# A new hand-laid order for the first half of an S4 convolution and gated feed-forward kernel

## The chip, the cores and the metric

The kernel runs on one core of a Trainium2 chip. The metric is device time in microseconds (us), from the start of the execution to its end. A core has five engines that matter here: PE (TensorE, matrix products), DVE (VectorE), ACT (ScalarE), POOL (GpSimd) and SP (SyncE, which here only starts transfers). Each engine works through its own list of instructions in a fixed order and waits on semaphores for the others. Transfers between HBM and the on-chip memory are started by SP, ACT or POOL and carried out by 16 DMA engines.

## The reference

One block of a network: a layer norm with a modulation, a long convolution whose kernel comes from a diagonal state-space model, and a gated feed-forward part. Sizes are L = 2048 positions, D = 448 channels, N = 256 complex states for each channel, Df = 1792.

```python
mod = silu(c) @ w_mod                      # six rows: sa ca ga sb cb gb
h = layernorm(x) * (1 + ca) + sa
# the convolution's kernel, 448 x 2048, from 256 complex exponentials each:
P = exp((dt * A)[:, :, None] * l)          # D x N x L
K = einsum("dn,dnl,dn->dl", Cc, P, dB).real
y = irfft(rfft(h, 2L) * rfft(K, 2L))[:L] + h * Dskip
x = x + ga * y
h = layernorm(x) * (1 + cb) + sb
x = x + gb * ((gelu(h @ w_gate) * (h @ w_up)) @ w_down)
```

## The kernel before

The work falls into two halves.

The first half, up to about 387 us, makes the convolution. The exponentials are never formed in full: a position is split into two factors (32 by 64), so that K is a product of two small tables for each channel. The channels go in 56 steps of eight. For a step, PE forms the arguments (`x.mm` L638, `y.mm` L657, `ang` L675) from rows `lt` that SP loads (`lt0`, `lt1`, L620; eight of each, seven steps use one), ACT takes the exponential (L644, L662) and sine and cosine (L688, L692, after an absolute value `mag` at L680 on ACT or L683 on DVE), DVE multiplies magnitudes with phases (`tx` L721, `ty` L725), and PE sums over the states (`kgen` L748). Every second step is drained (`kev`, L480 on ACT or L482 on DVE) and given the first pass of its Fourier transform (`ka`, L771). Beside this the input's transform runs (`ua`, `ub` L984, with stores `ub.st` of `us` at L1001). For the first two groups of channels, 160 each, the spectra are then multiplied and transformed back (`k_fft`: load of constants `f.fc` L1081, load of the input's spectrum `f.ut` L1087 and L1089, `f.fwd` L1094, `f.pr` L1098, `f.inv` L1105, drain `f.z`, store `f.st` L1113).

The last 128 channels follow at about 350 us in `t_fft` (products at L1197 and L1200, PE at L1189, L1207 and L1216). Its results go to memory twice: as `y` (L1231), and, for the first block of positions, as `yb_d` (drain `t.s0` by L480, store `t.st` L1224) so that the reload `yi.l` (L1297) of that block can begin early, batch by batch, nine batches of two transfers. The last stage of the convolution for the first block (L1409 and after) needs all of them.

The second half is the feed-forward part in four blocks of positions: gate and up products on PE (`gate_up`, L1524 and L1530), GELU on ACT, the product on DVE, and the down projection (L1599, L1630). `w.ld` (L1332) loads its weights, `yi.ld` (L1278) the later blocks of `y`.

What sets the order: every operation is registered as a task with `add(name, ...)`; `Task.__init__` (L275) takes its place from the table `PLACE` (L40 to L262), by name and running count. `Plan.order` sorts all 2006 tasks by place, and `Plan.run` emits them one by one. A letter behind a number names the engine where a task may go to more than one: a for ACT, d for DVE, p for POOL, s for SP. Each engine runs its instructions in the order in which they are emitted, and a transfer is an instruction of the engine that starts it. Nothing in the table is a wait: waits come from the data and from buffers that are used in turn. Places below 1480 are those ahead of the gate tiles of the second block of positions; the text calls the n-th task of a name (from zero) `name#n`.

```python
at = PLACE[n][i]
self.at, e = int(at.rstrip("adps")), at[-1]
...
out = sorted(self.tasks, key=lambda t: t.at)
```

Of the kernel before, what the change touches and what calls it, by code (L numbers as in the profile page):

```python
# [40 lines left out]
    "anc": "119 123 138 176 166 197 210 239 264 304 319 337 348 357 435 461 483 471 498 486",  # L41
    "ang": "113 108 132 150 164 172 203 208 233 303 318 332 345 355 426 460 478 441 497 473 510 582 605 595 665 679 657 694 "
        "743 751 766 787 783 801 773 876 878 916 894 903 938 934 1004 1023 1012 1033 1041 1047 1112 1126 1140 1145 1169 "
        "1176 1196 1201",
    "as": "69a 58a 101d 98d 121d 126d 174a 167d 251d 255a 280d 289a 311d 324d 334d 353a",
    "bn": "45 50 46 47 10 14 11 12 230 231 235 232 161 163 189 219",
    "c.ai": "1250",
    "c.ak": "201",
    "c.au": "57",
    "c.c": "16",  # L50
    "c.ea": "59",
    "c.ih": "1254",
    "c.ld": "21",
    "c.rd": "78",
    "c.t1": "236",
    "co.adde": "1338 1339 1355 1364",
    "co.addl": "1383 1391 1419 1416",
    "co.addx": "1495 1510 1499 1522 1672 1712 1735 1684 1791 1803 1809 1801",
    "co.ca": "1405a 1415a 1444a 1438a",
    "co.cb": "1413d 1418a 1454a 1447a",  # L60
    "co.h0": "1397a 1401a 1431a 1433a",
    "co.h2": "1534a 1580a 1571a 1562a 1748a 1744d 1755a 1760d 1848d 1882a 1833a 1866a",
    "co.l0": "1402 1411 1437 1445",
    "co.l2": "1541 1585 1573 1577 1749 1751 1757 1761 1849 1885 1843 1876",
    "co.mme": "1321 1317 1346 1347",
    "co.mml": "1374 1380 1417 1378",
    "co.mmx": "1492 1506 1494 1509 1636 1699 1731 1645 1784 1797 1804 1788",
    "co.n": "1396 1400 1429 1426",
    "co.nx": "1527 1575 1549 1532 1745 1742 1747 1759 1821 1868 1829 1863",
    "co.rc": "1393 1399 1428 1425",  # L70
    "co.rcx": "1525 1739 1820",
    "co.rt": "1384 1394 1427 1420",
    "co.rtx": "1524 1737 1810",
    "co.xt": "1542 1586 1574 1578 1750 1752 1758 1762 1850 1886 1851 1877",
    "co.ta": "1404 1410 1432 1434",
    "co.tb": "1407 1414 1443 1446",
    "cos": "521 588 634 616 689 704 686 708 754 760 769 792 791 819 813 886 899 932 909 923 953 954 1014 1034 1030 1054 1046 "
        "1052 1117 1139 1144 1153 1173 1190 1199 1222",
    "cos2": "122 124 145 179 169 200 212 245 269 313 326 338 349 359 439 463 484 472 505 488",
# [3 lines left out]
    "d0": "175",  # L83
# [21 lines left out]
    "dsk": "193",  # L105
    "dt": "24",
# [4 lines left out]
    "ev.end": "1247",  # L111
    "ev.fp": "697",
    "ev.geg": "1462",
    "ev.pq": "1334",
    "ev.ps": "1451",
    "ev.ub": "385",
    "ev.w0": "1333",
    "f.fc": "726 746 779 808 818 833 881 888 926 944 962 1020 1049 1074 1089 1119 1134 1152 1164 1191",
    "f.fwd": "727 759 786 809 821 850 884 892 930 950 966 998 1015 1028 1056 1075 1095 1120 1136 1160 1206 1218",
    "f.inv": "750 771 794 817 844 864 897 924 948 961 984 1008 1025 1053 1068 1086 1110 1131 1150 1182 1214 1230",  # L120
    "f.pr": "749 765 788 816 838 851 895 904 931 952 983 999 1016 1029 1067 1083 1096 1121 1149 1178 1213 1221",
    "f.st": "831 780 857 866 907 893 941 946 979 1007 1003 1044 1061 1077 1109 1124 1135 1170 1198 1205 1241 1281",
    "f.ut": "698 758 774 805 820 841 883 891 929 920 964 980 1006 1026 1055 1048 1080 1103 1122 1147 1185 1157",
    "f.z": "755a 772d 812d 832a 865a 887d 908d 928a 949a 986d 993d 1009d 1027d 1066d 1085a 1098d 1111a 1132a 1155a 1183a "
        "1219a 1233d",
    "gs": "64 77",
    "gu": "1479 1497 1511 1519 1528 1539 1550 1561 1570 1579 1592 1612 1618 1628 1640 1647 1656 1665 1674 1682 1690 1702 "
        "1708 1717 1769 1773 1776 1790 1792 1800 1808 1814 1822 1830 1835 1844 1853 1862 1895 1898 1901 1907 1912 1919 "
        "1923 1929 1933 1946 1952 1958 1962 1969",
    "gu.g": "1430 1440 1448 1458 1467 1465 1473 1481 1502 1508 1521 1529 1540 1551 1563 1572 1582 1591 1600 1619 1629 1637 "  # L130
        "1650 1657 1666 1675 1683 1691 1705 1709 1718 1723 1774 1777 1785 1793 1798 1805 1816 1823 1831 1836 1845 1854 "
        "1867 1870 1899 1902 1908 1913 1920 1924 1930 1934 1947 1953 1960 1963 1970 1975",
    "gu.h0": "1478 1485 1515 1536 1558 1581 1595",
# [5 lines left out]
    "gu.m": "1439 1441 1456 1461 1469 1470 1476 1483 1505 1513 1526 1531 1546 1555 1565 1576 1590 1593 1605 1621 1633 1639 "  # L139
# [3 lines left out]
    "gu2": "1422 1423 1442 1457 1459 1464 1471 1472",  # L143
    "ka": "228 261 292 341 382 405 506 527 656 585 703 712 737 828 800 871 914 943 970 989 1057 1076 1125 1165 1187 1210 "
        "1237 1245",
    "kd": "227 250 291 340 374 404 450 504 590 577 700 711 736 827 798 863 902 927 968 988 1040 1072 1102 1148 1186 1209 "
        "1236 1239",
    "kev": "218d 224a 290d 317a 373d 394d 448a 490a 548d 569d 699d 707d 735d 806d 797d 858a 900a 918a 960d 975a 1037a 1071d "
        "1101a 1138a 1166a 1195a 1235a 1238d",
    "kgen": "141 177 191 216 253 277 271 316 300 360 375 393 414 419 476 485 520 535 552 563 626 643 669 690 715 718 748 763 "  # L150
        "777 790 815 830 855 885 910 911 933 959 955 974 1018 1019 1045 1065 1081 1099 1129 1133 1156 1163 1175 1193 1204 "
        "1220 1224 1232",
    "kout": "229a 266a 299d 342a 442d 407a 507a 544a 658a 598a 710a 738d 739a 843a 804a 877d 917a 945d 976a 994a 1070d 1094a "
        "1130a 1167a 1188a 1211a 1244d 1246a",
    "lt0": "61 112 302 369 561 744 852 1017",
    "lt1": "95 162 384 432 742 745 965 1060",
    "m.cp": "553a 604a 793d",
    "m.cp0": "41d",
    "m.ev": "42 63 68 568 614 799",
    "m.ld": "27 36 17 433 558 761",  # L160
    "m.mm": "34 52",
    "m.mq": "549 603 776",
    "m.mq0": "20",
    "m.sm": "554 613 795",
    "m.sm0": "55",
    "mag": "518a 587a 610a 597d 670a 680d 664a 705a 752d 756a 767a 789a 784a 810a 775a 879a 889d 921a 905a 913a 939a 935a "
        "1010a 1031a 1013d 1038a 1042a 1050a 1116d 1127a 1142a 1146a 1171a 1177a 1197a 1202a",
    "norm": "66 70 93 67 118 65 89 110 234 252 273 243 320 307 308 350",
    "p.A1": "2 90 314 502",
    "p.A2": "3 91 330 508",  # L170
    "p.A3": "25 154 346 487",
    "p.B1": "6 107 354 543",
    "p.B2": "22 149 391 580",
    "p.B3": "23 151 427 629",
    "p.C1": "28 102 420 500",
    "p.C2": "32 103 421 607",
    "p.D1": "29 142 418 581",
    "p.E1": "38 171 446 639",
    "p.E2": "39 199 491 684",
    "p.E3": "43 205 492 685",  # L180
    "p.G1": "35 128 436 615",
    "p.S1": "5 104 331 542",
    "p.S2": "8 114 366 565",
    "p.S3": "9 125 390 579",
    "p.S4": "37 168 444 638",
    "p.al": "1 15 259 451",
    "p.c0": "26a 159d 428d 632d",
    "p.c1": "44a 241d 511a 729d",
    "p.d0": "30 183 429 660",
    "p.d1": "53 309 539 807",  # L190
    "p.e0": "31d 240d 458a 678d",
    "p.e1": "56d 321a 584d 845d",
    "p.f0": "40 244 459 730",
    "p.f1": "60 322 611 875",
    "p.ld": "0 7 86 87 170 265 368 452",
    "p.put0": "49 301 475 814",
    "p.put1": "85 323 674 901",
    "pad": "48 247 181 695",
    "rcp": "54 248",
    "rstd": "51 242",  # L200
# [1633 lines left out]
```

## Time and profile before

| what | us |
|---|---|
| median of 3 runs | 783.3 |
| lowest and highest of them | 781.65, 783.98 |
| the profiled execution's own time | 783.97 |
| its span in the profile | 782.0 |
| PE, DVE, ACT busy in the span | 728.2, 590.7, 459.6 |

The profiled execution's own time lies 0.67 us above the median of the runs. Its span runs from the first to the last recorded instruction; 2 us lie around it. The share of an engine that is busy is an average over stages that differ much: in the first half three engines are near full at once, in the second PE alone. So the readings below go by stretch of the span. Rows of a timeline hold the start in us, the duration, the engine, the line and operation, and in brackets the idle time ahead of it with what ended it; an engine's name with a q (SPq, ACTq) is the issue of a transfer by it. Rows of the stretches hold, for each engine, the busy time and the number of instructions, then the clock that PE was granted (1 is full) and the load on the DMA engines. Rows of the chain of waits hold start, duration and what ran.

### The profile page before, as it was taken

Reading aid. Unit: us, or ns where it says so; the run is one execution under the profiler, and the core shown is the slowest. Engines: PE = TensorE matmul, PEld = TensorE weight load, DVE = VectorE, ACT = ScalarE, POOL = GpSimd, SP = SyncE. Lnnn points to the kernel's source line nnn. Section 1 sums busy time; section 2 is a strip of 40 time slices with the busy share of each in tenths; the row PEclk is TensorE's granted clock in tenths of the full one; section 3 lists DMA queues with packets and bytes.
Section 4 is the critical chain, followed back from the end, with each engine's and each line's share of the span. In section 5 each row is a group of like instructions: output and inputs, shape, how many; then the busy total and the mean of one; then the engine's idle time right before and its main releaser. Section 6 shows DMA issues by size and latency. Waiting matters only on the chain.

```text
span 782.0 us, 19039 instructions
## 1 busy us (share of the span) xinstructions
PE 728.2 (93%) x8166; PEld 443.6 (57%) x8166; DVE 590.7 (76%) x889; ACT 459.6 (59%) x615; POOL 8.4 (1%) x23
## 2 busy tenths in 40 slices
PE   3677889998899999989999999999999999999998
PEld 1234444444577777677774445444694446944477
DVE  6999999999899999979767952569774587034743
ACT  5899998999899999862554730233411334022330
POOL 0000000000000000001200000000000000000000
PEclk9999999999999999999999999999999999999999
DMA  8645569998887598888876884355337224013201
GB/s 264 190 140 177 143 159 273 254 300 248 210 237 243 161 258 244 238 303 238 253 234 227 281 217 132 130 177 168 140 66 224 95 95 135 14 48 98 79 2 60
DMA packets 103950, 139.87 MB, mean 179 GB/s; under 512 B 34388, under 2 KB 85492, under 8 KB 103866
## 3 DMA queue, kind: packets, MB, share of 16 engines
q1 hardware_dynamic: 100436, 132.53, 57.8%
q10 hardware_dynamic: 2950, 5.38, 2.1%
q8 instruction: 64, 1.05, 0.6%
q0 software_dynamic: 480, 0.75, 0.3%
q14 instruction: 20, 0.16, 0.1%
HBM read 100.39 MB, written 36.01 MB: 174 GB/s over the span
## 4 chain that ended last, share of the span: by engine, by line
PE 66%; ACT 9%; DMA 8%; DVE 7%; issue 3%; SPq 2%; ACTq 0%; POOL 0%; DVEq 0%; POOLq 0%
PE pq L1530 24%; PE pq L1630 9%; PE pf L1105 5%; PE pg L675 4%; PE kg L748 4%; PE pd L1599 4%; PE pf L1094 3%; PE kg L771 2%; DMA w<-in_wgu 2%; PE pq L1524 2%; PE pd L1630 2%; ACT fg L688 1%; ACT my L662 1%; PE pf L984 1%; DVE ty L725 1%
## 5 line engine op out<-in xcount | busy, mean ns | idle before, releaser
L1530 PE MATMUL pq<-ht,wr 128*128 128x512 f16 (+1 forms) x1200 | 248.5, 365 | 0.4 <-DMA ht<-hl 0.4
L1530 PEld LDWEIGHTS <-wr 128*128 128x128 f16 x1200 | 114.5, 98 | 128.5 <-issue 11.8
L725 DVE TENSOR_TENSOR ty<-my,fg 128x2048 f32<-128x2048 f32 x56 | 127.6, 2281 | 0.0
L1537 ACT ACTIVATE ge<-pq 128x512 f32<-128x512 f32 (+1 forms) x60 | 33.8, 565 | 102.1 <-PE pq L1524 64.3
L1544 DVE TENSOR_TENSOR fq<-ge,pq 128x512 f32<-128x512 f32 (+1 forms) x60 | 38.9, 649 | 72.3 <-PE pq L1530 44.3
L1556 ACT ACTIVATE hh<-fq 128x1024 f16<-128x1024 f32 (+1 forms) x49 | 46.7, 961 | 65.0 <-DVE fq L1544 46.4
L721 DVE TENSOR_TENSOR tx<-mx,fg 128x1024 f32<-128x1024 f32 x56 | 67.8, 1216 | 4.4 <-ACT fg L692 3.0
L1630 PE MATMUL pq<-d,hh 128*128 128x224 f16 x476 | 68.9, 259 | 0.0
L748 PEld LDWEIGHTS kg<-ty,tx 128*32 128x32 f32 x3584 | 52.8, 110 | 21.6 <-issue 13.4
L748 PE MATMUL kg<-ty,tx 128*32 128x64 f32 x3584 | 61.5, 220 | 3.5 <-issue 1.6
L1559 DVE TENSOR_TENSOR hlo<-fq,hh 128x1024 f16<-128x1024 f32 (+1 forms) x49 | 53.7, 1106 | 13.4 <-ACT hh L1556 13.3
L1630 PE MATMUL pq<-d,hlo 128*128 128x224 f16 x238 | 61.7, 259 | 0.0
L688 ACT ACTIVATE fg<-pg 128x1024 f32<-128x1024 f32 x56 | 57.8, 1037 | 2.1 <-DVE tx L721 2.0
L662 ACT ACTIVATE my<-pg 128x1024 f32<-128x1024 f32 x56 | 55.5, 1033 | 3.7 <-PE pg L657 3.1
L1630 PEld LDWEIGHTS <-hh 128*128 128x128 f16 x560 | 54.2, 98 | 0.9 <-issue 0.2
L1105 PE MATMUL pf<-q,fc 128*128 128x160 f32 x264 | 43.4, 314 | 1.0 <-DVE q L1098 0.7
L1105 PEld LDWEIGHTS pf<-q,fc 128*128 128x128 f32 x264 | 37.5, 194 | 7.8 <-issue 4.7
L692 ACT ACTIVATE fg<-fg,small 128x1024 f32<-128x1024 f32 x36 | 41.4, 1170 | 0.1
L675 PEld LDWEIGHTS <-lt 64*128 64x128 bf16 x304 | 18.0, 94 | 37.1 <-issue 24.0
L675 PE MATMUL pg<-ea,lt 64*128 64x512 bf16 x152 | 31.4, 388 | 6.9 <-ACT fg L688 2.1
L1747 ACT ACTIVATE d<-fq 128x896 f16<-128x896 f32 x14 | 13.3, 947 | 39.8 <-PE pd L1599 27.3
L680 ACT ACTIVATE fg<-pg 128x1024 f32<-128x1024 f32 x30 | 31.1, 1037 | 2.0 <-PE pg L675 1.7
(208 smaller groups left out, 1121.8 us busy)
## 6 DMA issues: line engine op xcount, KB each, us to landing
wr<-w_d SPq DMA_DIRECT2D x21, 896.0 KB
fc<-in_k_fc SPq DMA_DIRECT2D x20, 576.0 KB
u_d<-so SPq DMA_DIRECT2D x32, 224.0 KB
ui<-u_d SPq DMA_DIRECT2D x10, 672.0 KB
fq<-in_wd SPq DMA_DIRECT2D x14, 448.0 KB
w<-in_wgu SPq DMA_DIRECT2D x11, 512.0 KB
us<-uo SPq DMA_DIRECT2D x22, 240.0 KB
q<-us SPq DMA_DIRECT2D x22, 240.0 KB
```

The source lines that it names most:

```text
L662: A.activation(yb.tile.rearrange("p h (n k) -> p n h k", n=2), pb.tile.rearrange("p (n h k) -> p n h k", n=2, h=2), AF.Exp)
L675: T.matmul(pa[:, nh * 512:nh * 512 + 512], w, x, start=(k == 0), stop=(k == 2))
L688: A.activation(fb.tile[:, 0].rearrange("p x (n k) -> p n x k", n=2), pb.tile.rearrange("p (n x k) -> p n x k", n=2, x=2), AF.Sin, scale=TW ...
L692: A.activation(fb.tile[:, 1], fb.tile[:, 1], AF.Sin, scale=-TWO_PI, bias=halfpi)
L721: V.tensor_mul(tx.tile, xb.tile[:, xm, None, :].to_broadcast([128, 2, 512]), fb.tile[:, :, 0])
L725: V.tensor_mul(ty.tile, yb.tile[:, :, None, :].to_broadcast([128, 2, 2, 512]), fb.tile[:, None, :, 1].to_broadcast([128, 2, 2, 512]))
L748: T.matmul(kg[32 * g:32 * g + 32, 2 * (s % 2) + q, :64], tx[:, r, nh, 4 * q + g], ty[:, 0:4:3, nh, 4 * q + g] if r else ty[:, 1:3, nh, 4 * ...
L1105: T.matmul(pz.tile[:, e % 32 - sl0], fc.tile[:, i, 1 + t], pp.tile[:, t, i], start=(t == 0 and e != 32), stop=(t == 1 and e != 0))
L1530: T.matmul(pb.tile[k][:, ts], wr.tile[:, 4 * lo + t, k, c0:c0 + 128], ht[:, m, ts], start=f % 2 == 0 and i == 0, stop=f % 2 == 1 and i == 9)
L1556: A.activation(hg.tile[0][:, cb, c], fq.tile[:, c], AF.Copy)
L1559: V.tensor_sub(hg.tile[1][:, cb, c], fq.tile[:, c], hg.tile[0][:, cb, c])
L1630: T.matmul(bank(k)[:, m], x[:, p, q[0], ts], w[:, p, q[1]], start=new and m == 0 and p == 0 and z == 0, skip_group_check=True, stop=i in ( ...
```

## The change

Only the table `PLACE` differs. 1422 of the 2006 tasks have another place, all of them below 1480; from there on nothing moves. 73 of them also have another engine (ACT instead of DVE or the other way). No task is added or taken away and no tile changes its size. Counted in tasks ahead of the end of `kgen`, ACT has two more `f.z`, one more `kev`, one more drain of `ua`, two more of `ub` and one more `mag`; DVE has two more `as` (scaling of the input, L909 on ACT and L911 on DVE) and one more `m.cp`. Table loads on ACT, which stand between functions of different kinds, go from 43 to 42.

An extract of the table:

```diff
-    "f.fc": "726 746 779 808 818 833 881 888 926 944 962 1020 1049 1074 1089 1119 1134 1152 1164 1191",
+    "f.fc": "729 750 776 790 816 841 874 881 918 929 954 1030 1054 1070 1078 1115 1135 1155 1177 1205",
...
-    "lt1": "95 162 384 432 742 745 965 1060",
...
+    "lt1": "90 119 393 387 697 769 1002 1046",
```

Three places, as the engines' lists have them. The first is SP ahead of `f.fwd#0`, the first product of the two spectra, whose constants are `fc`; `us` is the input's spectrum, `q` its reload, `lh_d` a padding row in memory. Before:

```order
L1001 DMA us_66<-uo 128x3x128
L514 DMA lh_d<-in_k_one 224x512
L1087 DMA q<-us_64 128x480
L1089 DMA q<-us_64 64x480 x2
L1081 DMA fc<-in_k_fc 128x1152
L620 DMA lt<-lh_d 64x7x128 x6
L1081 DMA fc<-in_k_fc 128x1152
```

Now:

```order
L1001 DMA us_66<-uo 128x3x128
L1087 DMA q<-us_64 128x480
L1089 DMA q<-us_64 64x480 x2
L620 DMA lt<-lh_d 64x7x128 x2
L1081 DMA fc<-in_k_fc 128x1152 x2
L805 DMA fg<-in_w_mod 112x1792
L1087 DMA q<-us_64 128x480
```

The padding row and four of the six `lt` transfers now stand further behind, the other two `lt` stand ahead of `fc`, and the second `fc` follows the first at once. `f.fwd#0` itself goes from place 727 to 732, behind two more `y.mm`.

The second is SP some 25 us earlier in the program, where `lt0#4` is loaded. Before:

```order
L971 DMA fu<-in_k_fc 128x3x128
L805 DMA fg<-in_w_mod 112x1792
L620 DMA lt<-lh_d 64x7x128 x2
L975 DMA ui<-u_d 128x3x448
L971 DMA fu<-in_k_fc 128x3x128
L1001 DMA us_64<-uo 128x3x160
```

Now:

```order
L1001 DMA us_64<-uo 128x3x160
L1001 DMA us_65<-uo 128x3x160
L1001 DMA us_66<-uo 128x3x128
L620 DMA lt<-lh_d 64x7x128 x2
L971 DMA fu<-in_k_fc 128x3x128
L975 DMA ui<-u_d 128x3x448
```

`lt0#4` goes from place 561 to 638, behind the stores `ub.st#6` of the input's spectrum; its first use, a `y.mm`, goes from 644 to 643.

The third is ACT at the end of the convolution: `z` is the drained result of one batch, `yb_d<-z` its store, `yi<-yb_d` a reload. Before:

```order
L480 ACTIVATE z_5181<-pf 128x128
L480 ACTIVATE z_5194<-pf 128x128
L1297 DMA yi<-yb_d 2x2x512
L480 ACTIVATE z_5215<-pf 128x128
L1224 DMA yb_d<-z_5194 128x128
L1224 DMA yb_d<-z_5215 128x128
L480 ACTIVATE lh<-pf 96x512
L1231 DMA y_69<-lh 96x4x128
L480 ACTIVATE z_5240<-pf 128x128
L480 ACTIVATE z_5254<-pf 128x128
L1224 DMA yb_d<-z_5254 128x128
```

Now:

```order
L480 ACTIVATE z_5173<-pf 128x128
L1224 DMA yb_d<-z_5173 128x128
L480 ACTIVATE zo<-pf 96x512
L480 ACTIVATE z_5212<-pf 128x128
L480 ACTIVATE z_5224<-pf 128x128
L1224 DMA yb_d<-z_5224 128x128
L480 ACTIVATE z_5260<-pf 128x128
L1224 DMA yb_d<-z_5260 128x128
L1345 ACTIVATE wr<-w 128x4x256
L1297 DMA yi<-yb_d 2x2x512
```

The reload on ACT (`yi.l1#2`, place 1313, now 1354) stood between two drains and ahead of all three stores on ACT; it now stands behind the last of them. On POOL, which before issued eight reloads, a store of `y`, two reloads and two stores, one store now comes first, then ten reloads in a row, then two stores.

336 rows, old and new, of the table PLACE are left out of this document.

## The prediction

> **What bounds the kernel now.** I read the stretches of the span first, because the shares over the whole span mix two different halves. The columns are: window and its length, busy time of PE, weight loads, DVE, ACT and POOL with their instruction counts, granted clock of PE, load on the DMA engines, GB/s.
>
> ```profile
> core 0: us, PE busy (x) PEld busy (x) DVE busy (x) ACT busy (x) POOL busy (x), PEclk, DMA share, GB/s
> 40.00:320.00 280.00, 256.54 (x4623) 159.48 (x4626) 272.10 (x322) 271.87 (x337) 0.00 (x0) 0.99 0.78 221
> 320.00:350.00 30.00, 25.96 (x607) 20.38 (x608) 24.74 (x25) 20.32 (x27) 0.00 (x0) 0.94 0.82 253
> 350.00:387.00 37.00, 34.59 (x383) 29.00 (x381) 31.38 (x61) 13.59 (x30) 6.82 (x12) 1.00 0.81 246
> 387.00:465.00 78.00, 77.41 (x480) 41.43 (x479) 58.05 (x97) 43.97 (x68) 0.69 (x1) 1.00 0.79 244
> 465.00:782.00 317.00, 313.11 (x2009) 184.93 (x2007) 173.11 (x312) 82.35 (x115) 0.00 (x0) 1.00 0.35 105
> ```
>
> Two things are to be seen. From 387 us on, PE idles 0.59 us of 78 and then 3.89 of 317. The change does not touch the work after 465, so that part keeps its length, and the time follows the moment at which the feed-forward part's first products start. Everything that can be won or lost lies before about 387. There, from 40 to 320, DVE and ACT are both full: DVE idles 7.90 us (280 − 272.10) and ACT 8.13. A new order can win little more than such idle time, or shift work between these two engines.
>
> Second, I looked where this idle time sits. The granted clock leads there.
>
> ```profile
> 112.00:116.00 4.00, 2.11 (x72) 1.15 (x65) 4.00 (x5) 4.00 (x6) 0.00 (x0) 1.00 0.70 150
> 196.00:200.00 4.00, 1.79 (x12) 1.21 (x11) 4.00 (x6) 2.62 (x4) 0.00 (x0) 0.95 1.14 176
> 199.40:202.80 3.40, 3.40 (x25) 2.39 (x26) 2.47 (x3) 1.76 (x2) 0.00 (x0) 0.52 0.82 192
> 325.90:328.90 3.00, 3.00 (x12) 1.89 (x13) 3.00 (x4) 1.02 (x1) 0.00 (x0) 0.50 0.80 212
> ```
>
> From 199.4 to 202.8 the clock is 0.52 and PE is busy throughout, so it does some 1.6 us less work than it would at full clock (3.40 × 0.48). What stood ahead of it shows in the queues of SP, PE and DVE, with one row of the chain of waits (the third):
>
> ```profile
> 192.31 0.53 SPq L1081 DMA_DIRECT2D fc<-in_k_fc  x1
> 192.89 5.87 SPq L620 DMA_DIRECT2D lt<-lh_d  x6
> 192.31 6.64 DMA fc<-in_k_fc
> 199.00 1.46 PE L1094 MATMUL pf<-ako,fc 128*128 128x160 f32 x6 [1.86 <-DMA fc<-in_k_fc]
> 204.23 1.22 DVE L683 TENSOR_SCALAR fg<-pg 128x1024 int32<-128x1024 int32 x1 [2.36 <-PE pg L675]
> 208.18 1.22 DVE L721 TENSOR_TENSOR tx<-mx,fg 128x1024 f32<-128x1024 f32 x1 [0.53 <-ACT fg L692]
> ```
>
> PE waits 1.86 us for the constants of `f.fwd#0`, runs the next 3.4 us at half clock, and DVE runs dry for 2.36 us behind it and 0.53 us once more. Of DVE's 7.90 us of idle time, 2.36 therefore have one named cause.
>
> Third, the end of the convolution, from the timelines of ACT, POOL and PE, with two rows of the chain of waits (those that name DMA).
>
> ```profile
> 363.32 0.28 ACT L480 ACTIVATE z<-pf 128x128 f32<-128x128 f32 x1 [0.33 <-PE pf L1216]
> 365.02 1.21 ACTq L1297 DMA_DIRECT2D yi<-yb_d  x1
> 366.37 1.10 ACTq L1224 DMA_DIRECT2D yb_d<-z  x2
> 369.18 0.34 ACTq L1224 DMA_DIRECT2D yb_d<-z  x1
> 366.37 2.63 DMA yb_d<-z
> 369.29 3.81 POOL L1297 DMA_DIRECT2D yi<-yb_d  x7 [2.94 <-DMA yb_d<-z]
> 373.63 1.08 POOL L1297 DMA_DIRECT2D yi<-yb_d  x2
> 370.38 4.67 DMA yi<-yb_d
> 378.85 0.44 PE L1409 MATMUL pd<-yi,ai 128*64 128x128 f32 x4 [1.23 <-DMA y<-lh]
> ```
>
> ACT drained a batch at 363.32 and then sat on a reload until 366.23 (365.02 + 1.21), with its stores queued behind it. POOL's reload waited for the store issued at 366.37, which landed at 369.00, and POOL then issued nine reloads one after another, about 0.54 us each (3.81/7 and 1.08/2). The last was issued at 374.17 or so; 4.67 us more is 378.84, which is when PE began. The row names `y<-lh`, but the reload's own sum fits the start to a hundredth, so I take the reload as what PE waited for.
>
> **The change, part by part.** The sum is made against the profiled execution: 783.97 us, of which the span is 782.0.
>
> A. Engines and tables. The durations:
>
> ```profile
> L482 DVE COPY zo<-pf 128x480 f32<-128x480 f32 x10 | 6.5, 649 | 0.2
> L480 ACT ACTIVATE zo<-pf 128x480 f32<-128x480 f32 x10 | 5.9, 587 | 2.6 <-PE pf L1105 2.6
> L482 DVE COPY ke<-kg 128x252 f32<-128x252 f32 x14 | 5.7, 410 | 0.8 <-PE kg L748 0.7
> L482 DVE COPY so<-pf 128x448 f32<-128x448 f32 x15 | 8.8, 616 | 1.5 <-PE pf L921 1.5
> L683 DVE TENSOR_SCALAR fg<-pg 128x1024 int32<-128x1024 int32 x6 | 7.3, 1218 | 2.5 <-PE pg L675 2.4
> L680 ACT ACTIVATE fg<-pg 128x1024 f32<-128x1024 f32 x30 | 31.1, 1037 | 2.0 <-PE pg L675 1.7
> L911 DVE TENSOR_SCALAR as<-au,rs 128x128 f32<-128x128 f32 x10 | 2.7, 278 | 0.8 <-PE pf L921 0.8
> L909 ACT ACTIVATE as<-au,rs 128x128 f32<-128x128 f32 x6 | 2.5, 424 | 0.4 <-DVE rs L889 0.4
> L662 ACT ACT_TABLE_LOAD x9 | 11.5, 1283 | 0.2
> ```
>
> DVE gives up two `f.z` (2 × 0.649), one `kev` (0.410), three drains of `ua` and `ub` (same 128 by 448 form, 3 × 0.616) and one `mag` (1.218): 4.77 us. It takes two `as` (2 × 0.278) and one `m.cp` (0.616, same form of copy): 1.17. Net −3.6. ACT takes two `f.z` (2 × 0.587), one `mag` (1.037) and the four smaller drains, which I set at DVE's price as an upper bound (2.26): 4.47. It gives up two `as` (0.85) and one table load (1.28): net +2.3 at most. If DVE alone set the pace of the 280 us, this would win 3.6; if ACT alone did, lose 2.3. Their idle times differ by 0.23 us, so neither is nearer, and I take the middle: **−0.6**. Both ends stay for the range.
>
> B. The wait for `fc`. In the new order SP no longer issues the padding row ahead of `fc` but issues two `lt` there. Six `lt` took 5.87, so two take 2.0, and `fc` would be issued up to 1.4 us later (2.0 less the padding's slot of about 0.6). In return four `lt` no longer share the DMA engines with it; their load was 1.14 from 196 to 200, over full, and `fc` took 6.64 to land. A load of `lt` in a thinner stretch, 21.99 to 25.13 in the next rows, took 3.1. `f.fwd#0` also comes two `y.mm` later, about 0.8 us of PE at 0.39 each (the pair of products at 174.84, below). If `fc` lands in 3.1 the wait is gone, and with it the half clock and DVE's 2.36: −2.4. If it still takes 6.64 it is later by 1.4 − 0.8, so +0.6. The four transfers taken away are most of what crowded it, so I lean to the first end: **−1.5**.
>
> C. The tail. Without the reload ahead of them ACT's stores can go out about 2.9 us earlier (366.23 − 363.32, less a drain). POOL is then free earlier, and the last reload hangs on the last store alone. That store, at 369.18, is set by PE and DVE, not by the reload; it lands 2.63 later at 371.8, its reload is issued in 0.54 and lands 4.67 later: 377.0, against 378.85. That is 1.8 earlier. PE idles 2.41 us from 350 to 387 (37 − 34.59), which no reordering here can beat without moving its work, so −2.4 is the end on the good side. On the other, if the last store comes two reload issues (0.54 each) later because drains and stores stand in another order, it costs +1. I take **−1.5**. The weight loads and `yi.ld` move past each other on SP after 390; they cost nothing as long as PE's 0.59 us of idle time from 387 to 465 stays, and that cover is the queue of gate products behind them.
>
> D. New waits. Transfers that had much reserve now have little. The sharpest is `lt0#4`:
>
> ```profile
> 150.11 1.26 SPq L620 DMA_DIRECT2D lt<-lh_d  x2
> 166.37 1.48 SPq L1001 DMA_DIRECT2D us<-uo  x3
> 174.84 0.39 PE L657 MATMUL pg<-ea,lt 64*128 64x512 bf16 x2
> 21.99 1.35 SPq L620 DMA_DIRECT2D lt<-lh_d  x2
> 25.13 0.39 PE L657 MATMUL pg<-ea,lt 64*128 64x512 bf16 x1 [0.65 <-DMA lt<-lh_d]
> ```
>
> It was issued at 150.11 for a product at 174.84. Now it follows `ub.st#6`, which ended at 167.85; with 3.1 us to land it is there at 171.0. The reserve falls from 21.6 us to 3.8. `lt1#6` goes from place 965 to 1002, one ahead of the `ang` that needs it. I take **0**, since 3.8 is still more than nothing; bounded by the wait below, up to +6.0.
>
> Sum: −0.6 − 1.5 − 1.5 + 0 = −3.6, so 780.4 as an execution of the profiled one's kind. That one lies 0.67 over the median, so against the median of 783.3 I forecast **779.7**, 0.5% faster.
>
> **The rivals.**
>
> *A late transfer (slower).* If SP gets to `ub.st#6` more than 3.8 us later in relation to PE than it did, the `y.mm` behind `lt0#4` waits, and `kgen` and all of PE's list behind it; `lt1#6` would do the same. A wait of a full landing is 3.1. With DVE's gap after such a wait (2.36 and 0.53, together 2.9) it is 6.0. Then B only moved its stall elsewhere: −0.6 + 0 − 1.5 + 6.0 = +3.9, so 787.9, less 0.67: **787.2**. For it: two such placements, and the sample of `fc`, where 6.7 us of lead were too little. Against it: 3.8 us of reserve, and single waits of DVE and ACT are hidden where the tiles ahead are buffered.
>
> The Trainium skill, "TensorE: Matmul & The Clock Gate", section "Part 1: The HAM clock gate (the "warmup" mystery)", says that PE's clock drops to half after at least one idle window of about 3.4 us and returns after about 3.4 us of sustained work. The trace agrees on the length (0.52 over 3.40 us, 0.50 over 3.00). On the cause it agrees less: 196 to 200 with 1.79 us of PE work in 4 led to a dip, 112 to 116 with 2.11 did not, so a window need only be thin, not empty. By the page's wording a wait of 3.1 us would cost 3.1 and no dip, and this rival would end near 784.3.
>
> *No change.* ACT sets the pace of the full stretch, so A is +2.3, `fc` keeps its 6.64 and B is +0.6, and the tail wins its 1.5: +1.4 at worst; with B at zero +0.8, so 784.8, less 0.67: **784.1**. For it: ACT takes on work at 271.87 of 280. Against it: the chain behind the stall at 199 runs over PE and DVE.
>
> *A larger gain.* All good ends at once: −3.6 − 2.4 − 2.4 = −8.4, so 775.6, less 0.67: **774.9**. It asks that DVE alone bounds the full stretch and that no wait is new.
>
> **How the numbers follow.** A change under about 0.3% (2.35 us) cannot be told from none here. Chances: forecast 0.48, with its own range 777.5 to 781.5; no change 0.26; late transfer 0.18; larger gain 0.08. Faster (below 780.95) takes nine tenths of the forecast's case and the larger gain, 0.52; slower (above 785.65) the late transfer and a little of the no-change case, 0.20; the rest, 0.28, is the same. The range goes from 774.9 to 786.6: it leaves out the upper half of the late transfer and what lies beyond all good ends, about one in eight.
>
> **What would show it.** A: from 40 to 320, DVE busy by 3.6 less and ACT by some 2 more. B: no dip of the clock at about 199 and no PE wait for `fc` before L1094. C: no gap on ACT behind a reload near 364, and the first L1409 1.5 us earlier than 378.85 counted from the end of `kgen`. D: no row of PE at L657 or L675 with a wait for `lt` between 165 and 290. The forecast is wrong if such a row stands there, if the dips only changed place, or if DVE's idle time from 40 to 320 stays near 7.9 although it has less to do: then the work moved and the end did not.

## The result and the profile after

| kernel | median, us | range, us | ratio to before, 95% interval |
|---|---|---|---|
| before | 783.64 | 781.65 to 784.61, 4 runs | |
| changed | 792.32 | 789.1 to 794.07, 4 runs | 1.0109 [1.0069, 1.0150] |
| changed, beside the kernels of the third group below | 788.83 | 787.04 to 792.71, 9 runs | 1.0059 [1.0032, 1.0086] |
| changed, beside those of the fourth group | 788.05 | 785.75 to 793.01, 12 runs | 1.0054 [1.0033, 1.0075] |

The change made the kernel slower, by 0.5 to 1.1%, which is 4 to 9 us. Single runs of one kernel spread more than the first four showed: the kernel before ran from 779.9 to 789.67 in 35 runs on one chip. A profile is one such run, so a difference of 2 us between two profiles is read with care, and the verdicts come from the ratios. A ratio is not the quotient of two medians (for `front_only` below, 782.52 and 785.55 would give 0.9961, and its ratio is 0.9984); where nothing else is said, differences in us are worked out from the ratio.

The stretches of the changed kernel's span (columns as before):

```profile
core 0: us, PE busy (x) PEld busy (x) DVE busy (x) ACT busy (x) POOL busy (x), PEclk, DMA share, GB/s
40.00:320.00 280.00, 252.86 (x4666) 158.33 (x4663) 271.14 (x321) 272.38 (x338) 0.00 (x0) 1.00 0.76 217
199.40:202.80 3.40, 3.31 (x76) 2.33 (x67) 3.18 (x5) 3.40 (x6) 0.00 (x0) 1.00 1.08 330
350.00:387.00 37.00, 28.29 (x321) 23.61 (x320) 26.29 (x49) 7.87 (x17) 6.96 (x12) 0.95 0.77 215
465.00:789.40 324.40, 320.45 (x2044) 188.19 (x2042) 176.21 (x316) 84.84 (x118) 0.00 (x0) 1.00 0.36 109
```

From 40 to 320 little moved: DVE has 0.96 us less to do, ACT 0.51 more. The dip of the clock at 199.4 is gone. From 350 to 387 PE idles 8.7 us where it idled 2.4. Three starts cut the span into pieces. The last `kgen` product stood at 346.5 us and now stands at 345.5; the first product of the convolution's last stage (L1409) at 378.85, now 384.85; the first gate product (L1530) at 387.4, now 395.1. From there to the end it is 394.6 and 394.4 us. So the front half won 1.0 us, and 8.7 were lost in the 41 us behind it: 7.0 ahead of L1409 and 1.7 behind.

The same stretch around the first and the last of these starts, first in the kernel before, then in the changed one:

```profile
335.00:345.00 10.00, 9.00 (x181) 7.39 (x179) 10.00 (x9) 7.50 (x10) 0.00 (x0) 1.00 0.87 296
345.00:355.00 10.00, 8.63 (x144) 8.08 (x145) 6.55 (x13) 2.47 (x4) 0.00 (x0) 1.00 0.93 311
355.00:365.00 10.00, 9.37 (x145) 7.89 (x145) 9.67 (x17) 2.02 (x8) 0.00 (x0) 1.00 0.69 184
```

```profile
335.00:345.00 10.00, 8.82 (x252) 7.84 (x244) 9.47 (x10) 8.25 (x11) 0.00 (x0) 1.00 0.53 178
345.00:355.00 10.00, 9.28 (x142) 8.73 (x130) 5.76 (x12) 3.17 (x5) 0.00 (x0) 1.00 1.03 328
355.00:365.00 10.00, 9.47 (x123) 7.68 (x125) 9.73 (x16) 1.53 (x6) 0.67 (x1) 1.00 0.98 243
385.00:390.00 5.00, 5.00 (x28) 3.70 (x29) 4.21 (x13) 1.07 (x3) 0.00 (x0) 0.50 0.60 170
```

The last two columns tell the story. Before, the DMA engines moved 2.96 MB from 335 to 345 (296 GB/s for 10 us) and had room from 355 to 365, load 0.69. Now they move 1.78 MB in the first window and are full in both that follow. Of the 1.18 MB less, 0.17 are made up from 345 to 355 and 0.59 from 355 to 365, just when the small stores of the batches are to go. SP's timeline shows why it was not moved, with one row of SP's waits and one of PE's timeline:

```profile
332.86 0.42 SPq L1140 DMA_DIRECT2D fg<-in_k_ft  x1
340.61 0.33 SPq L486 DMA_DIRECT2D idenh<-in_k_ih  x1
341.94 0.42 SPq L486 DMA_DIRECT2D ai<-in_k_ai  x1
SPq L486 <- PE pg L638: 7.2, 1, 7.2
340.29 0.28 PE L638 MATMUL pg<-rd,lt 64*128 64x256 bf16 x2
```

`idenh` is a 32 KB identity matrix (`c.ih`). Its memory comes free when the last `x.mm` has run, which is at 340.57 (340.29 + 0.28). The change moved it from place 1254 to 1243, ahead of seven loads for the last channel group that had stood ahead of it, and SP sat 7.2 us on it with those loads behind.

Then the tail, from the timelines of POOL, SP, ACT and PE in the changed kernel:

```profile
359.35 0.67 POOL L1231 DMA_DIRECT2D y<-zo  x1 [357.84 <-DMA yi<-y]
359.68 8.63 SPq L1224 DMA_DIRECT2D yb_d<-z  x4
366.54 0.59 ACT L480 ACTIVATE zo<-pf 96x512 f32<-96x512 f32 x1 [6.25 <-DMA y<-zo]
368.35 0.92 SPq L1332 DMA_DIRECT2D w<-in_wgu  x2
370.60 0.91 SPq L1224 DMA_DIRECT2D yb_d<-z  x2
375.06 5.19 SPq L1297 DMA_DIRECT2D yi<-yb_d  x6
384.85 1.12 PE L1409 MATMUL pd<-yi,ai 128*64 128x128 f32 x8 [6.51 <-DMA my<-in_k_ft]
395.09 2.13 PE L1530 MATMUL pq<-ht,wr 128*128 128x256 f16 x18
```

and from its chain of waits:

```profile
359.35 7.11 DMA y<-zo
370.60 5.97 DMA yb_d<-z
```

POOL's 48 KB store takes 7.11 us to land, and ACT waits 6.25 us for the buffer it empties, with three drains and their stores behind. The last two stores go out at 370.60, behind two 512 KB weight loads, and the chain has 5.97 us for a store there, where one of the same size, 64 KB, took 2.63 in the kernel before. The reloads follow, PE waits 6.51 us, and its clock is 0.50 from 385 to 390. (The row names `my<-in_k_ft`; SP's last reload, issued shortly ahead of it, fits as well.)

POOL's store was under way while SP's loads filled the engines. The Trainium skill says in "DMA: Bandwidth & Descriptors", section "Issuing engines are not separate DMA queues", that transfers started by different engines run on the same 16 DMA engines and interleave. The trace agrees for most of POOL's 7.11 us: up to 364 the load was 0.94 or more in every microsecond. From 364 to 366 it was 0.48 and 0.14 and the store had still not landed; what held it there is open.

### The profile page after: what moved, and what is told of

Read it like the earlier page. It is cut to its first block, busy times and chain, and to the rows that moved or that the text cites. A ratio compares the mean times of both kernels' runs of the same rounds, so it can differ in the third digit from the quotient of the medians.

```text
span 789.5 us, 19041 instructions
## 1 busy us (share of the span) xinstructions
PE 725.9 (92%) x8166; PEld 444.7 (56%) x8166; DVE 589.7 (75%) x890; ACT 459.9 (58%) x613; POOL 8.4 (1%) x23
## 4 chain that ended last, share of the span: by engine, by line
PE 50%; issue 46%; DMA 3%; SPq 0%; ACT 0%; DVE 0%; POOL 0%; ACTq 0%; POOLq 0%
PE pq L1530 30%; PE pq L1630 9%; PE pd L1599 4%; PE pq L1524 2%; PE pd L1630 2%; DMA w<-in_wgu 1%; PE pd L1404 1%; DMA y<-zo 1%; DMA yb_d<-z 1%; PE pf L1207 1%; DMA my<-in_k_ft 1%; PE pd L1409 0%; SPq L1297 0%; PE pq L1035 0%; PE pd L1690 0%
## 5 line engine op out<-in xcount | busy, mean ns | idle before, releaser
L1530 PE MATMUL pq<-ht,wr 128*128 128x512 f16 (+1 forms) x1200 | 248.5, 366 | 0.6 <-ACT ht L480 0.6
L1530 PEld LDWEIGHTS <-wr 128*128 128x128 f16 x1200 | 114.6, 98 | 129.0 <-issue 11.8
L1556 ACT ACTIVATE hh<-fq 128x1024 f16<-128x1024 f32 (+1 forms) x49 | 46.7, 961 | 66.0 <-DVE fq L1544 47.4
L688 ACT ACTIVATE fg<-pg 128x1024 f32<-128x1024 f32 x56 | 57.5, 1039 | 0.7 <-PE pg L675 0.6
L1105 PE MATMUL pf<-q,fc 128*128 128x160 f32 x264 | 41.5, 307 | 0.0
L675 PE MATMUL pg<-ea,lt 64*128 64x512 bf16 x152 | 31.3, 386 | 8.2 <-ACT fg L688 2.7
L675 PEld LDWEIGHTS <-lt 64*128 64x128 bf16 x304 | 17.9, 94 | 36.2 <-issue 22.8
L771 PE MATMUL kg<-ak,ke 128*64 128x128 f32 x448 | 30.6, 279 | 2.8 <-issue 1.4
```

What stands on the lines that cost most here:

```text
L675: T.matmul(pa[:, nh * 512:nh * 512 + 512], w, x, start=(k == 0), stop=(k == 2))
L688: A.activation(fb.tile[:, 0].rearrange("p x (n k) -> p n x k", n=2), pb.tile.rearrange("p (n x k) -> p n x k", n=2, x=2), AF.Sin, scale=TW ...
L1105: T.matmul(pz.tile[:, e % 32 - sl0], fc.tile[:, i, 1 + t], pp.tile[:, t, i], start=(t == 0 and e != 32), stop=(t == 1 and e != 0))
L1530: T.matmul(pb.tile[k][:, ts], wr.tile[:, 4 * lo + t, k, c0:c0 + 128], ht[:, m, ts], start=f % 2 == 0 and i == 0, stop=f % 2 == 1 and i == 9)
L1556: A.activation(hg.tile[0][:, cb, c], fq.tile[:, c], AF.Copy)
```

## The experiments

The last column of the table at the end of this section gives, for the one profiled execution of each kernel, the time from the last `kgen` product to the first gate product. It was 40.9 us before and 49.6 with the change.

**First group: which half, and which row.** The table `PLACE` can be cut: tasks up to some place in one order, all others in the other.

```diff
 # front_only
+order = [t for t in changed if place(t) < 1240] + [the rest, as before]
 # tail_only
+order = [t for t in before if place(t) < 1246] + [the rest, as changed]
```

> The change's order and engines up to the end of kgen, the order of before from the first product of the last channel group on. In the two profiles kgen ended 1.0 us earlier with the change, and the first gate product stood 7.6 us later. Theory T (the loss lies wholly behind the end of kgen): 782.6 us, in any case under 784.5. Rival F (the front half does not hold its gain, or sets the tail up badly): 785 or more.

Measured: 782.52 us (the kernel before beside it 785.55), ratio 0.9984 [0.9954, 1.0014]. As theory T expected.

> The order of before up to the end of kgen, the change's order from the first product of the last channel group on. Theory T: the whole loss is here, 791 to 794 us. Rival F: under 787.

Measured: 782.29 us, ratio 0.9988 [0.9958, 1.0019]. Theory T falls. The tail's order, which in the changed kernel loses 8.7 us, loses nothing behind the front half of before. Neither half is slow; only the two together are. What joins them is SP's list around the cut: in `tail_only` the loads for the last channel group stand in the part as before, ahead of the identity.

```diff
 # x_load_back (SP): the 896 KB load of x ahead of the reload of y
+L1265 DMA x<-in_A_u
 L1288 DMA yi<-y_67, y_68
 L1140 DMA fg<-in_k_ft
-L1265 DMA x<-in_A_u
 # zo_store_early (ACT): store of the first zo tile, place 1371, to behind 1291
```

> The changed kernel with one task moved: the 896 KB load of x for the first block stands ahead of the reload of y on SP again, as in the kernel before, not just ahead of the stores of the batches. Theory X (this load fills the DMA engines while the stores go out, so that they land after 7 us): at least half of the loss comes back, 785 to 788.5 us, and the first two stores on SP land in under 4 us. Rival Z (ACT's wait for a zo buffer is the cause): 790.5 or more.

Measured: 788.83 us, 1.0054 [1.0012, 1.0095]. That lies between the two theories.

> The changed kernel with one task moved: the store of the first zo tile goes out on ACT right behind its drain, as in the kernel before, so that the third zo drain has a free buffer and need not wait 6.25 us for POOL's store. Rival Z: 786 to 788.5 us. Theory X: the wait on ACT goes, but the last batch is drained at the same time (369.2 in both profiles), so at most 1.5 us come back: 790 or more.

Measured: 788.92 us, 1.0079 [1.0047, 1.0111], between the two theories again. Both kernels stay slower than before. By the profiles each took 3.7 us out of the 49.6, but the two later measurements of the changed kernel itself (1.0059, 1.0054) show that neither can be told from it.

**Second group: SP's last stores, the single moves together, and the prediction's terms B and C by themselves.**

```diff
 # sp_stores_first (SP)
-L1332 DMA w<-in_wgu x2
-L1297 DMA yi<-yb_d
 L1224 DMA yb_d<-z x2
+L1332 DMA w<-in_wgu x2
+L1297 DMA yi<-yb_d
 # three_moves: this, x_load_back and zo_store_early at once
 # before_act_reload (before, ACT): yi.l1#2 from 1313 to behind t.s0#7
 # before_fc_ahead (before, SP)
-L514 DMA lh_d<-in_k_one
 L1087, L1089 DMA q<-us
-L1081 DMA fc<-in_k_fc
-L620 DMA lt<-lh_d x6
-L1081 DMA fc<-in_k_fc
+L1081 DMA fc<-in_k_fc x2
+L620 DMA lt<-lh_d x2
+L514 DMA lh_d<-in_k_one
+L620 DMA lt<-lh_d x4
```

> The changed kernel with three tasks moved on SP: two 512 KB weight loads and one reload, which stood ahead of the stores of the batches 4 and 8, now stand behind them. Theory S (the last stores are issued 1.9 us late behind these and then land in 6.0 instead of 2.6 us because the weight loads fill the DMA engines): 5 us come back, 786 to 788.5 us, the two stores are issued at about 368.5 and land in under 4 us. Theory X (the load of x alone): at most 1.5 us come back, 790 or more.

Measured: 789.51 us, 1.0061 [1.0032, 1.0090]. Theory S falls: the 5 us do not come back. In this kernel's trace a store on the chain of waits lands in 1.61 us (issued on ACT at 369.13), and POOL's reloads go out from 370.82 on without a further wait for a store. But SP's own reloads now wait 3.2 us for a weight load, and PE waits 4.57 us ahead of L1409. So late stores are not the only way in which SP's list reaches PE.

> The changed kernel with all three single moves at once: load of x ahead of the reload of y, store of the first zo tile behind its drain, SP's last two stores ahead of the weight loads. If these three places hold the whole loss: 781 to 784 us. If the crowd comes from somewhere else (more reloads in a row on SP and POOL, other stores): 787 or more.

Measured: 790.45 us, 1.0062 [1.0039, 1.0086]. The three places do not hold the loss, alone or together, as long as what stands ahead of them stays.

> The kernel before with one task moved: the reload on ACT stands behind the last store on ACT, as in the changed kernel. This is term C of the prediction by itself, which said -1.5 us with bounds -2.4 and +1: 782.1 us. Rival (the last batch's own store sets the end, and POOL's queue is not late): within 0.7 of the kernel before.

Measured: 787.0 us beside 784.43, ratio 1.0009 [0.9982, 1.0035], that is +0.7 us by the ratio (+2.6 by the medians) with an interval of −1.4 to +2.7. Term C was −1.5. Rows of ACT's and PE's timeline from its profiled execution, the second slowest of ten (789.25 us):

```profile
367.65 0.28 ACT L480 ACTIVATE z<-pf 128x128 f32<-128x128 f32 x1 [1.01 <-PE pf L1216]
379.12 5.36 PE L1207 MATMUL pf<-my,fg 128*96 128x128 f32 x32 [2.06 <-DMA fg<-in_k_ft]
```

ACT no longer waits for the reload, as forecast, but a load of constants that stands behind the stores on SP is late in its turn, and PE waits 2.06 us for it. In this execution the stall went to another transfer of the same queue.

> The kernel before with SP's order around the first constants of the spectra changed as in the changed kernel: the padding row and four of the six lt loads go out behind both fc loads. This is term B of the prediction by itself, -1.5 us with bounds -2.4 and +0.6: 782.1 us, and no wait for fc ahead of the first L1094. Rival (DVE and ACT are full, what is won at 200 us is lost again before 350): within 0.7 of the kernel before although the wait is gone.

Measured: 783.67 us, ratio 0.9979 [0.9951, 1.0007]: −1.6 us, the size of term B, but not told from zero. The edit is not quite the change's: all six `lt` stand behind both `fc` here, where the changed kernel has two of them ahead. One row each of its PE timeline and of its stretches:

```profile
200.59 1.08 PE L1094 MATMUL pf<-ako,fc 128*128 128x160 f32 x6 [0.61 <-DMA fc<-in_k_fc]
```

```profile
196.00:200.00 4.00, 3.51 (x110) 2.77 (x100) 3.09 (x5) 3.35 (x5) 0.00 (x0) 0.67 1.07 320
```

The wait shrank from 1.86 to 0.61, and the six products behind it took 1.08 us, not 1.46: the clock was full there (1.00 from 200 to 204). The dip of the second row, 0.67 from 196 to 200, stands ahead of this wait, behind a thin stretch in which PE worked 1.42 of the 3 us from 192 to 195. So the stall that term B named went, and another dip stood beside it.

**Third group: the head of SP's queue.** (The changed kernel ran once more beside these; its numbers are in the first table.)

```diff
 # identity_back (changed kernel, SP)
-L486 DMA idenh<-in_k_ih
 L1138 DMA fg<-in_k_ft
 ... the loads for the last channel group, ai among them
+L486 DMA idenh<-in_k_ih
 L1288 DMA yi<-y_67
 # identity_early: front_only with the reverse move
 # identity_zo_x: identity_back with x_load_back and zo_store_early
```

> The changed kernel itself once more, beside the other three and the kernel before on one chip, because single runs of the same kernel differ by several us here. Both theories: 1.1% over the kernel before, some 6 to 9 us, and 49 to 50 us from the last kgen product to the first gate product.

Measured: 788.83 us, 1.0059, +4.6 us; 47.4 us from `kgen` to the gates. Slower again, but less than both theories had expected.

> The changed kernel with one row moved on SP: the 32 KB load of the identity matrix, for which SP waited 7.2 us until the last x.mm had run, stands behind the seven loads for the last channel group, not ahead of them. Theory H (this one wait at the head of SP's queue holds back some 1.7 MB, which then fill the DMA engines from 345 to 364, when the stores and reloads of the batches should go): most of the loss comes back, level with the kernel before or up to 3 us under it, the DMA share from 335 to 345 rises from about 0.5 to over 0.9, and the first gate product follows the last kgen product after 41 to 43 us, not 49.6. Rival O (the order of loads and stores behind it, which the single moves improved by 3 to 4 us each, is the cause): it stays 5 us or more over the kernel before.

Measured: 786.48 us, 1.0016 [0.9998, 1.0034]. The interval reaches from no loss to +2.7 us, so about 3 us came back, but theory H had expected the DMA engines full from 335 to 345, and their load was 0.72. SP's timeline and one row of its waits show that the next row had taken the place:

```profile
333.83 0.43 SPq L1150 DMA_DIRECT2D my<-us  x1
338.78 0.33 SPq L486 DMA_DIRECT2D ai<-in_k_ai  x1
SPq L486 <- PE pg L638: 4.4, 1, 4.4
```

`ai`, another 32 KB table, waits for the same product.

> The reverse: the kernel with the change's order up to the end of kgen and the order of before behind it, which ran level with the kernel before, with the load of the identity matrix as the only row moved, on SP, ahead of the loads for the last channel group. Theory H: SP waits some 7 us for the last x.mm again, and it becomes 4 to 9 us slower than without the move, 786.5 to 791. Rival O: within 1.5 us of the kernel without the move.

Measured: 784.06 us, 0.9991 [0.9968, 1.0014], beside 0.9984 for the kernel without the move. SP waited 6.6 us, as theory H had it, and the loads were held back as in the changed kernel:

```profile
335.00:345.00 10.00, 8.49 (x206) 7.36 (x204) 9.69 (x10) 7.66 (x11) 0.00 (x0) 1.00 0.61 205
345.00:355.00 10.00, 9.28 (x152) 8.61 (x141) 5.73 (x12) 3.17 (x5) 0.00 (x0) 1.00 1.01 367
```

Without the move 345 GB/s were moved in the first of these windows. Yet the time does not differ measurably: the wait alone, with the tail as before, is not the loss. (The two profiles differ by 2.8 us from `kgen` to the gates, so a smaller cost is not excluded.)

> The changed kernel with the identity load back, and two more moves: the first zo store behind its drain and the load of x ahead of the reload of y. Theory H: the two moves bring less than 1.5 us beside the first, so about the time of the kernel with the identity load back alone. Rival O: they bring 3 us or more.

Measured: 784.78 us, 1.0003 [0.9981, 1.0025]. The two moves brought 1.0 us by the ratios, as theory H expected, and 1.7 by the medians; neither is told from nothing.

**Fourth group: the whole wait, and the loads themselves.**

```diff
 # both_back (changed kernel, SP): idenh and ai behind the loads for the last channel group
 # loads_as_before: seven loads and one store at the places of before, ahead of idenh
 # both_back_three: both_back, and in addition
+L1265 DMA x<-in_A_u
+L1140 DMA fg<-in_k_ft
 L1288 DMA yi<-y_67, y_68
-L1140 DMA fg<-in_k_ft
-L1265 DMA x<-in_A_u
 #   and the store of the first zo tile behind its drain (ACT)
```

> The changed kernel with two rows moved on SP: the identity matrix and, in addition, the table ai, both 32 KB, which wait for the same last x.mm, stand behind the loads for the last channel group. With the identity alone moved, ai became the row at the head of the queue and SP still waited 4.4 us. Theory H (the waits at SP's head cause the loss): the DMA share from 335 to 345 is above 0.85, and the time is at most 1 us over the kernel before. Rival O (the later order): 2 us or more over the kernel before, as with the identity alone.

Measured: 787.31 us, 1.0038 [1.0015, 1.0062]. The DMA engines now moved 318 GB/s from 335 to 345, and 3.0 of the 4.2 us that the changed kernel lost on that chip are still there; the two intervals overlap. Rival O is right here: the wait is not the whole cause.

> The changed kernel with the seven loads for the last channel group (and one store) at the places in which the kernel before has them, ahead of identity and ai; front half and everything behind stay as changed. Among them is a 480 KB load that the change had put between the reload of y and the load of x. Theory L (the backlog of loads is the cause, whatever makes it): level with the kernel before or up to 3 us under it, 41 to 43 us from the last kgen product to the first gate product. Rival O: 3 us or more over the kernel before.

Measured: 783.88 us, 0.9995 [0.9972, 1.0018]. No loss, as theory L expected, and its interval lies apart from that of the changed kernel on the same chip, [1.0033, 1.0075]: eight rows of SP's list are enough to take the loss away. Its profiled execution was one of its slowest (786.37 us), with a stall ahead of L1409, so its 45.2 us in the table do not stand for the median.

> The changed kernel with identity and ai behind the loads, the load of x and a 480 KB load ahead of the reload of y, and the first zo store behind its drain. If backlog, load of x and zo wait each carry a part of the loss: 1 to 3 us under the kernel before, because the front half's 1 us is kept. If the single parts only trade places: 1 to 4 us over it.

Measured: 781.79 us, 0.9984 [0.9956, 1.0013]. No loss.

> The changed kernel itself beside these three on one chip: 4 to 9 us over the kernel before, by all theories.

Measured: 788.05 us, 1.0054, +4.2 us, as expected.

**Fifth group: two rows taken apart.**

```diff
 # fd4_only (changed kernel, SP)
+L1140 DMA fg<-in_k_ft
 L1288 DMA yi<-y_67, y_68
-L1140 DMA fg<-in_k_ft
 # three_but_waits (both_back_three, SP)
+L486 DMA idenh<-in_k_ih
 L1138, L1150 DMA fg<-in_k_ft, my<-us
+L486 DMA ai<-in_k_ai
 ... the other loads for the last channel group
-L486 DMA ai<-in_k_ai
-L486 DMA idenh<-in_k_ih
```

> The changed kernel with one row moved on SP: the 480 KB load that stood between the reload of y and the load of x goes out ahead of the reload of y. It is one of the rows that loads_as_before and both_back_three, the two kernels without a loss, share. If it is the row that counts: within 1.5 us of the kernel before. If the loss needs the waits at SP's head to go as well: 3 us or more over the kernel before.

Measured: 787.33 us, 1.0043 [1.0017, 1.0069]. It is not this row.

> The kernel without a loss (both_back_three) with identity and ai put back to the head of SP's queue, so that the wait of 7 us for the last x.mm is there again and all else is as in that kernel. Theory H in combination (the wait counts once the rest is in order): 3 us or more over the kernel before. Rival O (the wait is harmless, the order of the large loads is all): within 1.5 us of the kernel before.

Measured: 789.36 us, 1.0063 [1.0036, 1.0090]. This kernel and `both_back_three` differ in the places of two 32 KB loads on SP and in nothing else on any engine, and the two intervals, each against the kernel before on its own chip, lie apart. The stretches of `both_back_three`:

```profile
335.00:345.00 10.00, 8.83 (x242) 7.78 (x240) 8.55 (x9) 6.89 (x10) 0.00 (x0) 1.00 0.91 318
355.00:365.00 10.00, 9.51 (x145) 7.39 (x139) 9.76 (x15) 2.41 (x8) 1.58 (x3) 1.00 0.78 186
375.00:385.00 10.00, 8.32 (x82) 6.83 (x81) 7.71 (x25) 4.64 (x11) 0.00 (x0) 1.00 0.84 241
```

of `three_but_waits`:

```profile
335.00:345.00 10.00, 8.82 (x242) 7.84 (x242) 8.65 (x9) 7.56 (x10) 0.00 (x0) 1.00 0.52 175
355.00:365.00 10.00, 8.44 (x114) 7.00 (x111) 9.75 (x16) 1.65 (x7) 0.67 (x1) 1.00 0.86 205
375.00:385.00 10.00, 6.15 (x41) 4.66 (x40) 5.54 (x16) 2.72 (x5) 1.01 (x2) 0.72 0.65 180
```

and the two first products of the last stage, `both_back_three` first:

```profile
377.25 0.66 PE L1409 MATMUL pd<-yi,ai 128*64 128x128 f32 x8 [1.68 <-DMA my<-in_k_ft]
```

```profile
380.61 1.12 PE L1409 MATMUL pd<-yi,ai 128*64 128x128 f32 x8 [3.85 <-DMA my<-in_k_ft]
```

With the waits, 1.4 MB less is moved from 335 to 345, PE waits 3.85 instead of 1.68 us, and the clock falls, so that the same eight products take 1.12 instead of 0.66 us.

| kernel | ratio to before | `kgen` to gates, us |
|---|---|---|
| wait at SP's head, order behind as changed (three measurements) | 1.0109, 1.0059, 1.0054 | 49.6, 47.4, 46.3 |
| wait, single rows moved: x_load_back, zo_store_early, sp_stores_first, fd4_only | 1.0054, 1.0079, 1.0061, 1.0043 | 45.9, 45.9, 46.3, 45.0 |
| wait, several rows moved: three_moves, three_but_waits | 1.0062, 1.0063 | 48.6, 46.1 |
| wait, tail as before: identity_early | 0.9991 | 43.9 |
| most of the wait left on ai: identity_back, identity_zo_x | 1.0016, 1.0003 | 45.8, 45.8 |
| no wait, order behind as changed: both_back | 1.0038 | 45.3 |
| no wait, large loads early: loads_as_before, both_back_three | 0.9995, 0.9984 | 45.2, 40.6 |
| tail as before: front_only; front as before: tail_only | 0.9984, 0.9988 | 41.1, 40.9 |

Read together: the loss comes from SP's list between the last steps of `kgen` and the stores of the batches. Seven loads and a store put back ahead of the two waiting rows take it away, and the wait with it (`loads_as_before`). The wait for the last `x.mm` at the head of the queue is one part of it: two rows decide between `both_back_three` and `three_but_waits`. The order behind the wait is the other part: with the wait gone and that order as changed, `both_back` still loses 3.0 us, and with the whole tail of before the same wait brings no measurable loss (`identity_early`). The three moves of `three_but_waits` do not make the changed tail bear it: 4.9 us are lost there. Which rows of the tail of before do was not tried.

How the late loads reach PE is less sure. In the changed kernel's trace it is the landing of the stores, in `sp_stores_first` a weight load and SP's own reloads. How much belongs to the half clock behind the stall was not taken apart either. `both_back_three` is faster than the changed kernel (their intervals on one chip, [0.9956, 1.0013] and [1.0033, 1.0075], lie apart); against the kernel before, its 1.3 us cannot be told from nothing.

## Why the prediction was wrong

It forecast 779.7 us, with a range up to 786.6; the three measurements were 792.32, 788.83 and 788.05.

- **What bounds the kernel** held. The time followed the first gate product: 7.7 us later there (387.4 to 395.1), 7.5 us longer in the span. What was to be decided lay ahead of it.
- **A (−0.6)** and **B (−1.5)** together were to bring the end of `kgen` 2.1 us forward; in the profiles it came 1.0. The `fc` wait ahead of the first L1094 and its dip are gone in the changed kernel. `front_only` has both terms and measured −1.3 us, an interval that holds −2.1 and zero. Up to the end of `kgen`, DVE's busy time fell by 1.75 us (327.02 to 325.27), not 3.6, and ACT's rose by 1.44 (318.36 to 319.80), inside its bound of 2.3. One more 128 by 512 drain of `kgen` on DVE (`ako`, 6 to 7, about 0.7 us) had been left out of the count. From 40 to 320 DVE now idles 8.86 us (280 − 271.14), no less than before: the sign that the prediction had named for work that moves while the end does not.
- **C (−1.5, "+1" at worst)** is the step that failed. It came out at +8.7 us in the two profiles. The step took 2.63 us for a store and 4.67 us for a reload from the kernel before and held them fixed while it moved issues about on ACT and POOL. These durations are not prices: the kernel before has, in its chain of waits, another store of `z`, of only 16 KB, that took 4.92 us (row below) while the DMA engines were at a load of 1.02; the one of 2.63, 64 KB, had 0.64. In the changed kernel 64 KB took 5.97 us at 0.74, so the mean load does not set the time by itself. Nor did the reload's sum settle what PE waited for: the `y<-lh` that the row names, 375.63 + 3.22 us in the same chain, ends at 378.85 as well. And SP's list, which decides what runs beside a store, was read closely only at two other places. The rows that mattered stood in the order of SP's list: `c.ih` ahead of seven loads, the load of x and a 480 KB load behind the reload of y. The bound of +1 counted two reload issues and left out longer landings and later loads. By itself in the kernel before, the move on ACT brought nothing (`before_act_reload`).

```profile
360.03 4.92 DMA yb_d<-z
```

- **D (0)** was right at the places that it named: no product at L657 or L675 waits for `lt` in the changed kernel. The slower rival, a late transfer, was the right kind of event at the wrong place. Its 787.2 us came from `lt0#4`, which was in time.
- **The range** was too narrow at the upper end for the same reason as C, and the weight of the slower cases (0.20) was worked out from two named transfers, although 1422 tasks had moved and one queue's head was never checked for a wait on a late producer.
- On the clock, the rule weighed in the prediction was the Trainium skill's in "TensorE: Matmul & The Clock Gate", "Part 1: The HAM clock gate (the "warmup" mystery)": a fall behind an idle window of about 3.4 us. The trace agrees in the tail, where waits of 6.51 and 3.85 us led to 0.50 (385 to 390) and 0.72 (375 to 385) and one of 1.68 to none. It differs for two waits shorter than that, of 2.29 and 2.06 us, which the clock's fall to 0.50 followed as well, as the last section shows.

## What to carry to other kernels

Where a list of transfers is reordered, look first for any row, however small, that waits for a late producer, and count the bytes that stand behind it: they are moved later, into whatever comes then. The landing time of a small store depends on more than its size (here 2.63 to 7.11 us), so a duration read at one place is no bound for a stretch that the change may fill. And two halves of a schedule can each be harmless and cost 0.5 to 1% together, so test the halves before the rows.

## What the runs showed of the hardware

- While a load of 32 KB stood at the head of SP's queue and waited some 7 us for a product, 1.2 to 1.4 MB less was moved in the 10 us from 335 to 345: 178 against 296 GB/s in the changed kernel and the one before, 175 against 318 in `three_but_waits` and `both_back_three`, 205 against 345 in `identity_early` and `front_only`.
- In the changed kernel a store of 48 KB took 7.11 us to land, with the DMA engines full for its first 4.6 us and thinly loaded after; one of 64 KB took 5.97 us at a mean load of 0.74, behind two weight loads. In the kernel before, 16 KB took 4.92 us at 1.02 and 64 KB 2.63 us at 0.64.
- On SP a weight load waited, as the profile names it, for the landing of a `yb_d` store, with which it shares no data (waits of SP's queue, changed kernel: total, times, longest). What ties them was not tried.

```profile
SPq L1332 <- DMA yb_d<-z: 3.1, 1, 3.1
```

- The clock fell behind waits of little more than 2 us too. In `before_act_reload` it was 0.50 from 380 to 382, behind a wait of 2.06 us. In `identity_early` it was 0.50 from 380 to 383: four products took 0.44 us right behind a wait of 2.29 us, and four more of the same shape, 0.46 us later, 0.65 (rows below). Behind waits of 1.68 us (`both_back_three`) and 1.89 us (`tail_only`) it stayed full, yet behind the 1.86 us of the kernel before it fell, with PE busy for 1.79 of the 4 us from 196 to 200. So the length of the wait alone does not decide.

```profile
379.26 0.44 PE L1409 MATMUL pd<-yi,ai 128*64 128x128 f32 x4 [2.29 <-DMA my<-in_k_ft]
379.72 0.65 PE L1409 MATMUL pd<-yi,ai 128*64 128x128 f32 x4
```
